# Copying the chunk indicators on GpSimd (POOL) in place of VectorE (DVE), with a new order of every engine's queue

## Chip, cores and metric

One core of one Trainium2 chip. The metric is the device time of one execution in microseconds (us). The core has five engines that run side by side, each through its own list of instructions in order: PE (matrix products and transposes), ACT (activations, copies out of PSUM), DVE (elementwise work, reductions, copies), POOL (GpSimd, here casts, fills and selects) and SP (which issues nearly all DMAs). They wait for one another through semaphores.

## What is computed

Attention over selected chunks of keys, then a gMLP block with a residual. Cut to what matters:

```python
# q, k, v: (4, 8, 768, 64); chunks of 32 keys, nc = 24; top_k = 6
k_min, k_max = k_chunks.min(3), k_chunks.max(3)
ub = sum_d(maximum(q * k_min, q * k_max))         # a bound for each query and chunk
ub = where(chunk is causal, ub, -1e9)
sel = each query's 6 best chunks
scores = where(sel & causal, q @ k.T / 8, -1e9)
x = softmax(scores) @ v                           # heads side by side: (4, 768, 512)

h = gelu(x @ w_in)                                # (4, 768, 1024)
u, v_ = halves of h
v_n = (v_ - mean) / sqrt(var + 1e-6) * g_ln
out = x + (u * (w_sg @ v_n + b_sg)) @ w_out       # w_sg mixes the 768 positions
```

## The kernel before

**Work.** The 32 heads are taken as 16 pairs, p = 0 to 15; four pairs make a batch. The two heads of a pair lie on partitions 0 to 63 and 64 to 127. A pair goes through these steps (the words in brackets are the names that the code gives its operations):

- k and q are loaded, transposed on PE (`ktr`, `qtr`, L550, a half of 384 columns at a time), and copied out of PSUM by ACT or DVE (`kev`, `qev`, L450 on ACT, L453 on DVE). DVE reduces k to its minima and maxima per chunk (`kmm`, L578, four per pair) and subtracts one from the other (`wsub`, L597). The relu of q (`rel`) is done on DVE for pairs 0 to 3 (L619) and on ACT after them (L616); it reads both halves of the pair's qT. POOL casts q to bf16 into QA (`qcast`, L625) and v into vx (`vcast`, L635).
- The bounds are matmuls of q and relu(q) with the minima and differences (`ub`, L660 for pairs 0 to 3 one by one, L707 for later pairs two by two). The first form also reads the small tiles CMw and CMb, which POOL and ACT make at the start. DVE turns the bounds (L670), takes the best eight (L677), marks what lies below the sixth (L683) and turns the marks back into Dt (`dt`, L687).
- Scores are matmuls (`sc`) in pieces of at most 1024 PSUM columns, with two buffers in turn; ACT takes exp of each piece into E (`exp`, L849 for pairs 0 to 3, L801 after). POOL zeroes what lies above the diagonal (`aff`, L858, L806). For pairs 0 to 3 the selection enters the scores as further matmuls of Dt with IND (L840), so nearly every piece of their scores waits for Dt. For later pairs the marks stand in QA and the indicator stands in KA, beside q and k: a DMA (`qd`) brings Dt into QA, a copy of INDF into KA (`mrow`, L749 on DVE) or a DMA does the other.
- PE multiplies E with v (`pv`, L879, then the diagonal blocks `pvd`, L885), and DVE divides by the sums (`rcp`, L895; `xs`, L897) into XS.

After every fourth pair the batch goes through the gMLP: XS is transposed (`xtr`, L919, by DMA for some), x @ w_in (`hv`, L943; `hu`, L962), gelu on ACT, statistics on DVE (L952), a power on POOL (L984), the normalised vhat on DVE (L996), the mixing matmuls (`pt`, L1014), gate and product on DVE (L1031, L1035), the last matmuls (`ou`, L1047), the residual sum on DVE (L1056) and a store. While the first pairs run, w_sg is loaded, cast on POOL (L446), transposed on PE (L496) and copied out by DVE (L453), and w_in and w_out are loaded and cast (L446).

**The indicators.** IND is a bf16 tile of 128 x 2 x 768. On partitions 0 to 31, first plane, its row c is -480 in the 32 columns of chunk c and 0 elsewhere. POOL zeroes the tile (L397), DVE fills 32 rows (L399), POOL cuts them to the chunks with two selects (L401). The same 32 x 768 block is then needed at partitions 32 (plane 1), 64 (plane 0) and 96 (plane 1): three copies, on DVE at L412 when `INDV` is 1. DVE adds the planes to INDF (L417).

**Order.** Every operation gets a number as the program is written down. A table, `TABLE`, lists these numbers for each engine in the order in which the engine runs them, the PSUM buffer of every tile, and how many idle matmuls PE runs ahead of some operations (`filler`: seven ahead of the first transposes of k, four ahead of the first transpose of q, four ahead of the first transpose of pair 1's k). The program works out from the tables which waits are needed. With `shift=True` an operation on POOL also waits for the one ahead of it on POOL, and the one behind waits for it. Buffers that are freed late hold the loads that are to fill them: SP issues in order too.

Some numbers: 13, 14, 15 are the three copies, 16 is INDF; 9, 11, 12 make IND on POOL; 19 is CMw, 20 and 21 are CMb, 8 is identB, 4 to 7 small fills on POOL; 45, 49 are `ktr` and 54, 56 `qtr` of pair 0, 52, 48 its `kev` and 57, 55 its `qev`, 46, 47, 50, 51 its `kmm`, 53 its `wsub`, 58 its `rel`, 59 its `qcast`, 61 its `ub`; 81, 82, 85, 86 are `kmm` of pair 1, 94 its `qcast`. 65, 100, 123, 175 are Dt of pairs 0 to 3.

Of the kernel before, what the change touches and what calls it, by code (L numbers as in the profile page):

```python
# [256 lines left out]
def dmac(issue=530):  # L257
    return issue, issue


def _build(nc, ctx, q, k, v, w_in, g_ln, w_sg, b_sg, w_out, out):
# [4 lines left out]
    NT = S // 128  # L266
# [25 lines left out]
    P = Program()  # L292
# [12 lines left out]
    wsgT = T("wsgT", [128, NT, S], BF16)  # L305
# [17 lines left out]
    WSB = 1  # L323
    WSC = "pool"
# [4 lines left out]
    INDV = 1  # L329
# [51 lines left out]
    def idle(e):  # L381
# [7 lines left out]
         reads=["onesF"], writes=["identF"])  # L389
# [87 lines left out]
    def wsg_load(j):  # L477
# [4 lines left out]
        if WSB:  # L482
            sb = vh0[:, S * (j % 4):S * (j % 4) + S]
            if WSC == "pool":
                cast(sb, dst, S, ("wsc", j), [("stg", j % 4)] + names, [("stb", j % 4)])
            elif WSC == "dve":
                P.op("dve", lambda d: d.tensor_copy(sb, dst), dve(S, rate=2), ("wsc", j), port=True,
                     reads=[("stg", j % 4)] + names, writes=[("stb", j % 4)])
            else:
                P.op("act", lambda d: d.activation(sb, dst, ACTF.Copy), act(S), ("wsc", j),  # L490
                     reads=[("stg", j % 4)] + names, writes=[("stb", j % 4)])
            t = ps_g.tile((0, 1))
# [619 lines left out]
    for p in range(4, NP + 4):  # L1112
# [40 lines left out]
    "act": (  # L1153
# [11 lines left out]
    "dve": (  # L1165
# [99 lines left out]
```

## Time and profile before

| | us |
|---|---|
| median of 3 runs | 213.79 |
| lowest and highest | 213.75, 213.96 |
| the profiled execution | 213.85 |
| its span, first to last instruction | 212.1 |
| ahead of and behind the span | 1.75 |
| granted TensorE clock, share of full speed | 0.999 |

The page gives busy time, share of the span and count of instructions for each engine; its PEld is PE's loading of weights, beside its matmuls. The chain of work that ended last is followed back from the last instruction, at each step to what released it, and gives shares of the span by engine. The table of stretches gives, for each stretch from A to B, its length, the busy us and number of instructions of PE, PEld, DVE, ACT and POOL, PE's clock, the share of the DMA engines and GB/s. A row of the timeline is: start, duration, engine, line of the code, operation, tile written <- tiles read, shape; x3 means three such instructions in a row, and brackets give the engine's idle time ahead of them and what ended it.

### The profile page before, as it was taken

Reading aid. Unit: us, or ns where it says so; the run is one execution under the profiler, and the core shown is the slowest. Engines: PE = TensorE matmul, PEld = TensorE weight load, DVE = VectorE, ACT = ScalarE, POOL = GpSimd, SP = SyncE. Lnnn points to the kernel's source line nnn. Section 1 sums busy time; section 2 is a strip of 40 time slices with the busy share of each in tenths; the row PEclk is TensorE's granted clock in tenths of the full one; section 3 lists DMA queues with packets and bytes.
Section 4 is the critical chain, followed back from the end, with each engine's and each line's share of the span. In section 5 each row is a group of like instructions: output and inputs, shape, how many; then the busy total and the mean of one; then the engine's idle time right before and its main releaser. Section 6 shows DMA issues by size and latency. Waiting matters only on the chain.

```text
span 212.1 us, 5923 instructions
## 1 busy us (share of the span) xinstructions
PE 203.4 (96%) x2326; PEld 134.0 (63%) x2326; DVE 184.1 (87%) x537; ACT 158.5 (75%) x246; POOL 88.8 (42%) x119
## 2 busy tenths in 40 slices
PE   7989999889999999999999999999999999999993
PEld 3646677644767577776456767779646668545552
DVE  2999999879999899898799999899897887788894
ACT  2468999987599779998949989999977868256000
POOL 8424697795262645474121456465502311002000
PEclk9999999999999999999999999999999999999999
DMA  7999999992989998898989988826320007412007
GB/s 152 218 219 254 212 237 336 338 306 68 221 225 231 215 273 205 194 211 189 230 201 220 207 165 220 224 79 149 59 61 3 3 0 97 129 47 105 2 33 264
DMA packets 91339, 36.07 MB, mean 170 GB/s; under 512 B 84144, under 2 KB 86448, under 8 KB 91312
## 3 DMA queue, kind: packets, MB, share of 16 engines
q1 hardware_dynamic: 91024, 35.31, 73.7%
q8 instruction: 18, 0.29, 0.6%
q10 hardware_dynamic: 288, 0.39, 0.5%
q14 instruction: 9, 0.07, 0.1%
HBM read 24.77 MB, written 6.29 MB: 146 GB/s over the span
## 4 chain that ended last, share of the span: by engine, by line
PE 63%; DVE 23%; ACT 9%; issue 2%; POOL 1%; DVEq 0%
PE PSG L1014 15%; PE PSC L795 11%; PE PSG L1047 9%; PE PSG L943 7%; DVE W L578 6%; PE PSG L962 6%; ACT E L801 5%; PE PSG L550 5%; PE PSG L879 4%; DVE vhat L996 3%; DVE XS L897 2%; PE PSG L707 2%; ACT KA L450 2%; PE PSC L382 2%; PE PSG L885 2%
## 5 line engine op out<-in xcount | busy, mean ns | idle before, releaser
L801 ACT ACTIVATE E<-PSC 128x1024 bf16<-128x1024 f32 (+1 forms) x72 | 62.9, 917 | 7.8 <-PE PSC L795 7.6
L795 PE MATMUL PSC<-QA,KA 128*128 128x128 bf16 (+2 forms) x336 | 37.5, 246 | 0.4
L578 DVE TENSOR_REDUCE W<-PSG 128x12 f32<-128x384 f32 x64 | 32.7, 547 | 3.8 <-PE PSG L550 3.6
L1014 PE MATMUL PSG<-wsgT,vhat 128*128 128x384 bf16 x192 | 34.5, 326 | 0.4 <-DVE vhat L996 0.2
L806 POOL TENSOR_SCALAR_AFFINE_SELECT E<-E 128x768 bf16<-128x768 bf16 x24 | 21.1, 878 | 32.3 <-ACT E L801 31.9
L625 POOL CAST QA<-qT 64x768 bf16<-64x768 f32 (+1 forms) x28 | 24.1, 859 | 15.9 <-ACT qT L450 10.0
L795 PEld LDWEIGHTS PSC<-QA,KA 128*128 128x128 bf16 x336 | 24.1, 98 | 8.4 <-ACT E L801 2.4
L1014 PEld LDWEIGHTS PSG<-wsgT,vhat 128*128 128x128 bf16 x192 | 17.9, 98 | 12.5 <-ACT uT L968 1.3
L1047 PE MATMUL PSG<-woutb,uT 128*128 128x512 bf16 (+1 forms) x100 | 23.7, 371 | 0.0
L962 PE MATMUL PSG<-xT,winb 128*128 128x384 bf16 x128 | 23.6, 326 | 0.0
L1031 DVE SCALAR_TENSOR_TENSOR PSG<-PSG,glnT,bsgbc 128x384 f32<-128x384 f32 x32 | 19.7, 619 | 4.1 <-PE PSG L1014 3.9
L849 ACT ACTIVATE E<-PSC 128x1024 bf16<-128x1024 f32 (+3 forms) x26 | 21.2, 866 | 2.4 <-PE PSC L840 2.1
L943 PE MATMUL PSG<-winb,xT 128*128 128x512 bf16 x96 | 22.1, 379 | 0.6 <-issue 0.6
L968 ACT ACTIVATE uT<-PSG 128x384 bf16<-128x384 f32 x32 | 15.1, 490 | 10.0 <-PE PSG L962 9.7
L450 ACT ACTIVATE KA<-PSG 128x384 bf16<-128x384 f32 (+1 forms) x38 | 18.3, 492 | 3.7 <-DVE W L578 3.3
L879 PE MATMUL PSG<-vx,E 128*128 128x65 bf16 x480 | 19.9, 194 | 1.0 <-DVE XS L897 0.6
L635 POOL CAST vx<-vn 128x768 bf16<-128x768 f32 x16 | 13.3, 836 | 17.8 <-DMA vn<-in_v_dram 13.4
L879 PEld LDWEIGHTS PSG<-vx,E 128*128 128x128 bf16 x480 | 17.6, 97 | 3.6 <-DVE XS L897 1.5
L948 ACT ACTIVATE vgb<-PSG 128x512 f32<-128x512 f32 x24 | 13.2, 599 | 7.2 <-PE PSG L943 7.0
L1035 DVE TENSOR_TENSOR uT<-PSG,uT 128x384 bf16<-128x384 f32 x32 | 17.7, 555 | 0.9
L897 DVE TENSOR_TENSOR XS<-PSG,rden 128x384 bf16<-128x384 f32 x32 | 17.7, 554 | 0.9
L952 DVE BATCH_NORM_STATS2 stats<-vgb 128x6 f32<-128x512 f32 x24 | 15.8, 685 | 2.6 <-ACT vgb L948 2.5
(88 smaller groups left out, 328.8 us busy)
## 6 DMA issues: line engine op xcount, KB each, us to landing
kn<-in_k_dram SPq DMA_DIRECT2D x32, 192.0 KB, 4.6
qn<-in_q_dram SPq DMA_DIRECT2D x32, 192.0 KB, 4.5
vn<-in_v_dram SPq DMA_DIRECT2D x12, 384.0 KB, 5.2
out_dram<-osb SPq DMA_DIRECT2D x18, 256.0 KB, 2.4
vn<-in_v_dram SPq DMA_DIRECT2D x8, 192.0 KB, 4.8
uT<-in_moe_w_sg_dram SPq DMA_DIRECT2D x4, 384.0 KB, 6.2
vgb<-in_moe_w_in_dram SPq DMA_DIRECT2D x3, 512.0 KB, 6.1
KA<-INDF SPq DMA_DIRECT2D x12, 96.0 KB, 2.6
```

The source lines that it names most:

```text
L450: P.op("act", lambda e: e.activation(dst(), src(), ACTF.Copy), act(n), tag, reads=reads, writes=writes, ps=ps, shift=shift)
L578: P.op("dve", lambda d, m=m, op=op, src=src, h0=h0, h1=h1: d.tensor_reduce(W[w][:, m, 12 * h0:12 * h1].rearrange("p (h c) -> p h c", h=h1 ...
L625: P.op("pool", lambda g, i=i, r0=r0, r1=r1: g.tensor_copy(QA[w][i or 0][r0:r1, :], qT[r][r0:r1, :]), gps(S, 250 if i == 1 else 150), ("qca ...
L795: r = e.matmul(t.ap()[:, o:o + n], KA[w][i][:, 128 * kb:128 * kb + 128], QA[w][i][:, q0:q0 + n], start=True, stop=True)
L801: P.op("act", lambda e, t=t, c0=c0, c1=c1, i=i: e.activation(E[es][:, i, c0:c1], t.ap()[:, 0:c1 - c0], ACTF.Exp, scale=SCALE), act(c1 - c0 ...
L849: P.op("act", lambda e, t=t, c0=c0, c1=c1, n=n: e.activation(E[es][:, :, c0:c1], t.ap().rearrange("p (i x) -> p i x", i=2)[:, :, 0:n], ACT ...
L879: r = e.matmul(t.ap()[:, 65 * (qb - q0):65 * (qb - q0) + 65], E[es][:, i, at[kb, qb]:at[kb, qb] + 128], vx[w][:, kb, i, :], start=x == 0, ...
L897: P.op("dve", lambda d, pv3=pv3, nq=nq, rs=rs, q0=q0, q1=q1: d.tensor_tensor(XS[:, b % 2, hh // 2, q0:q1, i * DH:(i + 1) * DH], pv3()[:, : ...
L943: r = e.matmul(t.ap()[:, 0:F], xT[s][:, dk, 128 * qt:128 * qt + 128], winb[:, dk, F:DFF], start=(dk == 0), stop=(dk == NDK - 1), skip_grou ...
L962: r = e.matmul(t.ap()[:, 0:TG], winb[:, dk, 128 * fb:128 * fb + 128], xT[s][:, dk, TG * tg:TG * tg + TG], start=(dk == 0), stop=(dk == NDK ...
L1014: r = e.matmul(t.ap()[:, 0:TG], vhat[s][:, sb, 128 * fb:128 * fb + 128], wsgT[:, sb, TG * tg:TG * tg + TG], start=(sb == 0), stop=(sb == N ...
L1047: r = e.matmul(t.ap()[:, 0:n1 - n0], gT[s][:, fb, 128 * qt:128 * qt + 128], woutb[:, fb, n0:n1], start=(fb == 0), stop=(fb == NF - 1))
```

## The change

`INDV` goes from 1 to 2: the three copies of IND become POOL's `tensor_copy` (the branch stands in the code before already), each with `shift=True`. An option `WSD` for transposing w_sg by DMA is added and is off. The tables are new ones for all five engines, with new PSUM buffers, and the fillers stand at the same places in PE's list (two of them now named by the other half of the same transposes). The sets of operations are the same on every engine, but for 13, 14 and 15, which go from DVE's list to POOL's.

```diff
     WSB = 1
+    WSD = 0
     WSC = "pool"
...
-    INDV = 1
+    INDV = 2
...
     "pe": (
-        "1 45 49 54 56 84 80 61 91 188 89 103 107 196 192 96 190 194 166 198 112 114 242 159 200 155 246 250 "
-        "164 119 254 248 244 204 229 227 252 208 209 133 205 309 317 216 221 315 171 319 311 258 259 313 262 "
+        "1 49 45 54 56 80 84 61 91 188 89 103 107 196 192 96 190 194 166 198 112 155 159 242 114 200 164 254 "
+        "250 248 119 244 246 204 205 229 227 252 208 209 133 317 309 221 216 315 171 313 311 137 262 319 263 "
...
     "act": (
-        "22 23 52 55 48 57 83 92 189 90 87 197 193 191 195 199 243 201 247 251 162 255 249 245 158 230 228 "
-        "253 231 310 318 316 224 225 320 219 312 314 220 364 366 370 362 368 284 278 372 273 282 274 279 285 "
+        "23 52 57 55 48 22 83 92 189 90 87 197 193 191 195 199 243 201 255 251 249 158 245 162 247 230 228 "
+        "253 231 318 310 316 225 224 314 219 220 320 312 368 362 273 370 366 364 372 282 278 284 274 279 285 "
...
     "dve": (
-        "0 28 18 10 26 24 17 25 27 47 51 50 14 46 13 15 53 58 85 82 81 86 62 63 88 64 65 110 93 105 106 109 "
-        "16 108 104 97 98 113 99 111 100 167 115 116 160 161 157 165 156 120 121 122 168 163 266 123 210 212 "
-        "134 206 211 207 222 218 223 217 172 173 174 175 138 264 265 260 261 277 276 331 325 326 272 226 271 "
+        "0 25 27 17 18 10 26 28 24 50 51 47 46 53 58 82 85 81 86 62 63 64 88 65 110 93 106 104 105 109 97 16 "
+        "108 98 167 99 113 100 115 111 116 161 157 156 165 160 120 121 163 206 207 122 212 123 266 210 211 "
+        "168 223 218 222 217 134 172 173 138 174 175 264 272 265 260 271 261 276 277 331 325 326 280 226 329 "
...
     "pool": (
-        "9 386 215 334 2 3 269 19 11 4 12 20 21 6 7 5 8 59 94 202 203 213 117 60 169 132 267 233 257 95 256 "
-        "136 232 118 322 321 332 170 79 374 373 73 287 77 71 286 288 384 140 148 152 181 144 457 404 403 353 "
+        "386 9 4 215 2 334 3 20 7 5 11 12 21 13 15 19 8 6 59 14 269 94 202 203 213 117 60 132 169 267 232 257 "
+        "95 136 233 256 332 118 322 321 79 170 374 373 77 73 71 286 152 287 148 384 144 140 288 457 403 183 "
...
     "sp": (
-        "29 30 31 32 34 33 35 36 39 40 69 68 67 42 41 66 37 38 131 128 129 127 43 126 44 135 74 124 75 177 "
+        "29 30 31 32 34 33 35 36 40 39 66 68 42 69 41 67 37 38 131 128 129 126 127 44 43 135 74 75 176 177 "
...
     "filler": (
-        "45:7 54:4 84:4 "),
+        "49:7 54:4 80:4 "),
```

More of the change, by code (lines that the diff above doesn't have):

```diff
@@ L491, in wsg_load @@
                      reads=[("stg", j % 4)] + names, writes=[("stb", j % 4)])
+            if WSD:
+                P.op("sp", lambda e: e.dma_start_transpose(wsgT[:, :, 128 * j:128 * j + 128], sb), dmac(1300), ("wst", j),
+                     reads=[("stb", j % 4)] + [("vhat", 0, x) for x in range(NT)],
+                     writes=[("wsgT", j, hf) for hf in range(2)], dma=f"wt{j}", xfer=900)
+                return
             t = ps_g.tile((0, 1))
@@ L1134 @@
     "pe": (
[18 rows of a table removed]
-    "act": (
[11 rows of a table removed]
-    "dve": (
[18 rows of a table removed]
-    "pool": (
[13 rows of a table removed]
[18 rows of a table added]
+    "act": (
[11 rows of a table added]
+    "dve": (
[18 rows of a table added]
+    "pool": (
[13 rows of a table added]
     "slots": (
-        "0123021232033001111103211301001112301011000111023013323000101132100111010012301010102132032123220323"
-        "3232223333321100112210110011102310011001101032100001100132100101110303223203321332233232232221011013"
-        "2101000001132101010001011330110001110220111010032103310123213323323223233201011032010011320001112311"
-        "010022012320013111020122002331032103"),
+        "1023203010212331111110123201001112230301010011032012323010100123001110101103210010103220122230332323"
+        "2223233323230110013211001011003210000101110132101100100132100001130312022330121223333223322321000102"
+        "2100101111032100110110100321000100101331001101032110201031332332222223333201110022101100320001112311"
+        "000133103120301130012122121333000210"),
     "filler": (
-        "45:7 54:4 84:4 "),
+        "49:7 54:4 80:4 "),
 }
```

98 rows, old and new, of the table TABLE are left out of this document.

## The prediction

> **What bounds the kernel now.** I read the page's busy shares and its chain of work first, then the busy times by stretch, then the timeline of the stretches in which the engines of the chain change.
>
> ```profile
> PE 203.4 (96%) x2326; PEld 134.0 (63%) x2326; DVE 184.1 (87%) x537; ACT 158.5 (75%) x246; POOL 88.8 (42%) x119
> ...
> PE 63%; DVE 23%; ACT 9%; issue 2%; POOL 1%; DVEq 0%
> ```
>
> The shares alone would name PE. The chain says more: 23% of the span, some 49 us, hang on DVE, which is where the change takes work away. The stretches say when; their columns are busy us of PE, PEld, DVE, ACT and POOL.
>
> ```profile
> 5.00:10.00 5.00, 5.00 (x34) 3.40 (x36) 4.23 (x11) 2.19 (x5) 2.44 (x8) 1.00 1.35 218
> ...
> 35.00:40.00 5.00, 4.57 (x92) 3.60 (x92) 4.88 (x10) 5.00 (x7) 3.70 (x6) 1.00 1.08 355
> ...
> 60.00:65.00 5.00, 4.79 (x33) 3.00 (x32) 4.57 (x10) 4.95 (x8) 3.64 (x5) 1.00 0.88 213
> ...
> 200.00:205.00 5.00, 5.00 (x31) 2.84 (x29) 5.00 (x11) 0.00 (x0) 0.00 (x0) 1.00 0.00 2
> ```
>
> From 10 to 40 us DVE is nearly full (4.88 of 5 in the row shown); ACT joins it in the second half (5.00). Late in the kernel PE is full (200 to 205). So there are two kernels in a row: attention of the first pairs, paced by DVE and ACT, up to the first gMLP matmul, then a stage paced by PE. What the first stage saves moves the second one forward whole, as long as PE finds its inputs there; what is saved later off PE is worth nothing. Between 5 and 10 us, where the three copies stand, DVE is not full: 4.23 of 5.
>
> **The three copies.** The timeline of the first 14 us (start, duration, engine, line, operation, tiles):
>
> ```profile
> 4.48 0.82 POOL L401 TENSOR_SCALAR_AFFINE_SELECT IND<-IND 32x768 bf16<-32x768 bf16 x1
> ...
> 5.27 0.91 POOL L426 TENSOR_SCALAR_AFFINE_SELECT CMb<-CMb 64x288 bf16<-64x288 bf16 x2
> 5.66 1.59 DVE L578 TENSOR_REDUCE W<-PSG 128x12 f32<-128x384 f32 x3 [2.97 <-PE PSG L550]
> ...
> 5.98 1.51 PE L382 MATMUL PSC<-warm 128*128 128x512 bf16 x4
> ...
> 7.28 0.35 DVE L412 COPY IND<-IND 32x768 bf16<-32x768 bf16 x1
> ...
> 7.33 0.82 PE L550 MATMUL PSG<-identF,qn 128*128 128x128 f32 x6
> 7.64 0.56 DVE L578 TENSOR_REDUCE W<-PSG 128x12 f32<-128x384 f32 x1
> ...
> 8.23 0.72 DVE L412 COPY IND<-IND 32x768 bf16<-32x768 bf16 x2
> ...
> 8.62 0.49 ACT L450 ACTIVATE qT<-PSG 128x384 f32<-128x384 f32 x1
> ...
> 9.15 0.46 DVE L619 TENSOR_SCALAR rT<-qT 128x576 f32<-128x576 f32 x1
> 9.18 1.11 POOL L625 CAST QA<-qT 128x768 bf16<-128x768 f32 x1 [2.49 <-ACT qT L450]
> 9.52 1.94 DVE L578 TENSOR_REDUCE W<-PSG 128x12 f32<-128x384 f32 x4
> ...
> 10.99 1.73 SPq L528 DMA_DIRECT2D qn<-in_q_dram  x2
> ...
> 12.78 1.11 POOL L625 CAST QA<-qT 128x768 bf16<-128x768 f32 x1 [2.49 <-ACT qT L450]
> ```
>
> *Removed from DVE.* Three copies, 0.35 + 0.72 = 1.07 us. But behind them stands the relu of pair 0 (L619, 9.15), which reads the whole of qT, and ACT writes the second half of that from 8.62 to 9.11. ACT waits there for PE's transposes of q (7.33 to 8.15), and those stand behind four filler matmuls (L382, to 7.49) that the new table keeps in the same place. In the new order ACT takes the halves the other way round and ends at the same 9.11, because the later transpose ends at 8.15 whatever the order. So DVE finishes its four reductions near 7.75 (5.66 and four steps of about 0.52), the 24-column subtraction near 8, and then waits for 9.15: the 1.07 us turn into idle time. The reductions of pair 1 stand behind the relu in both orders and start at 9.52 as before. **I take the copies' removal at nothing.** What is late next there is ACT's qT, and behind it PE's fillers; bounds are 0 and 1.07.
>
> *Added to POOL.* No row shows POOL copying from one group of 32 partitions to another. The nearest row is its select of the same tile (L401, 32x768 bf16 to bf16): 0.82; the dearest 768-element cast is 1.11 (L625). I take 0.82, with 1.11 and, for a form never seen, twice the nearest, 1.64, as the upper end. POOL's rows before them end near 5.8 (the two selects of CMb, L426, end at 6.18 in the old order; the new one has 0.36 less ahead of them: a memset of 0.36 and CMw's select of 0.18 have gone behind, two small memsets of W have come forward), so two copies run from 5.8 to 7.5, then CMw, identB and one small memset until 8.35, then the cast of pair 0 (9.18 as before, since it waits for the same qT). That is 0.83 us of cover, 0.41 for each copy: up to 1.2 us each nothing moves. The third copy stands between that cast and the next one, in an idle 2.49 us less one memset of 0.41. The change makes each copy wait for the POOL instruction before it; that is the order it has anyway. CMw comes later on POOL (7.75 in place of 3.6) and its copy on ACT moves behind four evictions, to about 9.6; the first bound matmul, which reads it, needs the relu, to 9.61. Nothing, then.
>
> [...]
>
> **The new order up to the gMLP.** All engines get another sequence, so I walk it with the durations of the rows.
>
> ```profile
> 18.57 0.56 DVE L453 COPY qT<-PSG 128x384 f32<-128x384 f32 x1
> ...
> 19.53 0.48 DVE L687 STREAM_TRANSPOSE Dt<-Dn 128x288 bf16<-128x288 bf16 x1
> ...
> 26.55 0.48 DVE L687 STREAM_TRANSPOSE Dt<-Dn 128x288 bf16<-128x288 bf16 x1
> ...
> 27.14 0.39 DVE L749 COPY KA<-INDF 64x768 bf16<-64x768 bf16 x1
> ...
> 32.88 0.48 DVE L687 STREAM_TRANSPOSE Dt<-Dn 128x288 bf16<-128x288 bf16 x1
> ...
> 36.55 1.10 DVE L749 COPY KA<-INDF 64x768 bf16<-64x768 bf16 x1
> ...
> 42.85 0.56 DVE L897 TENSOR_TENSOR XS<-PSG,rden 128x384 bf16<-128x384 f32 x1
> ```
>
> ```profile
> 20.79 1.94 ACT L849 ACTIVATE E<-PSC 128x1024 bf16<-128x1024 f32 x2 [0.62 <-PE PSC L840]
> ...
> 27.68 2.90 ACT L849 ACTIVATE E<-PSC 128x1024 bf16<-128x1024 f32 x3
> ...
> 34.77 4.70 ACT L849 ACTIVATE E<-PSC 128x1024 bf16<-128x1024 f32 x5
> ...
> 40.08 0.39 ACT L849 ACTIVATE E<-PSC 128x256 bf16<-128x256 f32 x1
> ```
>
> *Masks.* The masked scores of a pair wait for its Dt (L687: 19.53, 26.55 and 32.88 for pairs 1 to 3). For pair 1 the new order puts one qT eviction ahead of it that stood behind it (0.37 more): Dt at 20.4 in place of 20.0, ACT's next exp at 20.9 in place of 20.79, but a small one comes first, and the half dozen ACT instructions behind it close up again to within 0.1. For pair 2 a reciprocal and a product XS (0.2 + 0.56) come ahead and two small vector instructions and a copy of 0.58 go behind: Dt ends at 27.17 against 27.03; ACT's exps of pair 2 start at 27.93 against 27.68, **0.25 lost**. For pair 3 the eviction of a w_sg block (0.56) comes ahead: Dt ends at 33.9 against 33.4; the exps of pair 3 start at 34.7 against 34.77, since ACT was the later one.
>
> *Gain at the end of the stage.* Before the last exp of pair 3 (40.08) the old order has a q and a k eviction that the new one puts behind it, and the new one has one k eviction instead: about 0.4 less. Five exps at 0.92 and one k eviction after 34.7 bring it to 39.65. POOL's two diagonal selects of pair 3 (0.86 each) now wait for that order's last but one exp, 39.75, and end at 41.5; the last product XS of pair 3 (42.85) ends at 42.75 in place of 43.41. ACT still has five evictions and the relu of pair 5 to do, to 42.85, before the bound matmuls of pairs 4 and 5; transposes, ACT's evictions of them, and the first gMLP matmul follow in the same steps as now.
>
> ```profile
> L446 POOL CAST winb<-vgb 128x1024 bf16<-128x1024 f32 x3 | 3.1, 1039 | 0.1
> ```
>
> ```profile
> 46.06 4.29 PE PSG L943 x19
> ...
> 57.51 2.75 DVE vhat L996 x6
> 60.38 2.11 PE PSG L1014 x12
> ```
>
> PE's first gMLP matmul (46.06) comes at about 45.55: **0.5 gained**. The weight casts it reads (POOL, L446) end at 44.7: after 41.5 three casts of 1.04.
>
> ```profile
> qn<-in_q_dram SPq DMA_DIRECT2D x32, 192.0 KB, 4.5
> ```
>
> ```profile
> 16.97 0.55 PE L550 MATMUL PSG<-identF,qn 128*128 128x128 f32 x3
> ```
>
> *DMA.* Loads are moved too: half of pair 3's q goes from the 11th load to the 14th, an issue in the row of 10.99, so by the 4.5 us of the page it lands at 15.5 to 16.4. PE reads it at 16.97, behind scores that wait for ACT in both orders, so nothing. SP's later loads (w_sg, w_out, q and k of pairs 6 to 8, the mask rows) change places among themselves; those that I followed still land ahead of PE's use.
>
> **The gMLP of batch 0 and after.** DVE's vhat (57.51 to 60.26) holds PE's first mixing matmul until 60.38, and PE is idle for 0.21 of the 5 us from 60 on, which is that wait. In the new order PE has two more small groups ahead of that point and the same work in all, and vhat, behind the last w_sg eviction, the variance and POOL's power, ends within 0.1 us of PE's readiness. So the **0.2** of waiting go. From there PE is full in both; the last 13 us have the same 14 groups and one more that moved in from before them. I take all later moves at zero, which is a choice: I followed them only at the tail and at batch 1's start.
>
> **Sum.** Copies 0, order before the gMLP -0.5, wait before the first mixing matmul -0.2: -0.7 on the profiled execution's 213.85 (span 212.1 and 1.75 around it), 213.15. The median of the runs is 0.06 lower, 213.79: **213.1**.
>
> ```profile
> 23.98 0.63 PE L879 MATMUL PSG<-vx,E 128*128 128x65 bf16 x15
> ...
> 26.76 0.34 PE L885 MATMUL PSG<-vx,E 128*128 128x65 bf16 x6
> ```
>
> ```profile
> 36.40 1.04 POOL L446 CAST winb<-xT 128x1024 bf16<-128x1024 f32 x1
> ```
>
> **Rivals.**
> *The copies count in full* (213.79 - 1.07 = 212.7). For it: DVE is the full engine of the next 30 us. Against: ACT's 9.11 ahead of the relu. 12%.
> *A lock eats the gain* (213.8). DVE's 64-partition copy of the indicator takes 0.39 in one place (27.14) and 1.10 where a POOL cast had just begun (36.55 against 36.40). In the new order one such copy stands directly ahead of pair 2's Dt, at 26.3, and POOL's cast for pair 4 starts at 26.45. If DVE is 0.15 us later than I think, the copy costs 0.7 more, and ACT, which then waits for Dt, passes all of it on: -0.7 + 0.7. 18%. [...]
> *A new wait ahead of a mask* (slower, 214.6). The product XS of head 0 now stands on DVE ahead of pair 2's Dt. It needs head 0's diagonal matmul on PE, at 26.76 to 27.10 in the old order, behind Dt's need. My walk has it done by 24.9, since PE takes it directly after the first part (23.98) and DVE comes by at 25.2. But PE gets there only after a score buffer is freed by ACT. If it ends later than 25.2, DVE, Dt, the scores and ACT wait one for another, us for us; as late as now, 27.1, it costs 1.9: 215.0. From 26.4 on (1.2) it is slower than before by over 0.2%: 214.3 to 215.0, the middle 214.6. 30%. The same form, an order that makes engines wait in a ring, can come anywhere in the 60 to 180 us that I took at zero, so it gets this much.
> *POOL's copies are dear.* Above 1.2 us each, the cast of pair 0 and everything behind it move by twice the excess: 0.9 us at 1.64, 214.0; 9%, half of it within 0.2%, half slower.
>
> **Chances.** My forecast has 31%. Faster by over 0.2% (about what a measurement of this kernel can tell from none, 0.43 us): forecast and first rival, 0.43. Within 0.2%: the lock and half of the dear copies, 0.22. Slower: the rest, 0.35. The forecast's own range is 212.8 to 213.4. The range given reaches from the full copies with a little of the rest, 212.4, to the full price of the new wait, 215.0.
>
> **What would show it.** Three POOL copies of IND, two between 5.8 and 7.5 and one after 10.2, of 0.82 each; DVE idle for about 1.1 us ahead of a relu that still starts near 9.15; the reductions of pair 1 at 9.5. Dt of pairs 1 to 3 ending near 20.4, 27.2 and 33.9. The last XS of pair 3 near 42.75, the first gMLP matmul near 45.5, the first mixing matmul near 59.7 to 60.0. Wrong is: the relu at 8.1 (first rival), an indicator copy of 1.1 us ahead of Dt (second), a gap on DVE ahead of the reciprocal of head 0 (third), POOL copies above 1.2 us (fourth), or PE idle in the later stages by more than now.

## Result and profile after

The changed kernel takes **214.9 us** (median of 11 runs, 214.14 to 216.06) against 213.79 (213.60 to 213.98) before: a ratio of 1.0049, 95% interval 1.0029 to 1.0069. It is slower, where 213.1 was forecast; the range, 212.4 to 215.0, holds the median by 0.1. The profiled execution took 215.11 with a span of 213.1. So 1.0 of its 1.26 us over the old profiled one lies in the span, and the time around the span grew from 1.75 to 2.01.

The page, busy times and chain:

```profile
PE 203.5 (96%) x2326; PEld 134.6 (63%) x2326; DVE 182.9 (86%) x534; ACT 158.6 (74%) x246; POOL 91.8 (43%) x122
...
PE 68%; DVE 16%; ACT 10%; DMA 2%; issue 1%; POOL 1%; SPq 0%; DVEq 0%
```

DVE has 1.2 us less to do than before and POOL 3.0 more; the chain's DVE share fell from 23% to 16%, PE's rose from 63% to 68%. By the chain alone this looks like relief for DVE. The stretches (same columns as before) show where DVE went the other way; the first row is the old kernel's from 30 to 35 us, the others are the changed kernel's:

```profile
30.00:35.00 5.00, 4.91 (x111) 3.48 (x100) 4.56 (x19) 4.85 (x9) 3.76 (x5) 1.00 1.13 288
```

```profile
5.00:10.00 5.00, 4.78 (x26) 3.47 (x26) 2.62 (x7) 2.31 (x6) 3.42 (x8) 1.00 1.15 218
...
25.00:30.00 5.00, 4.94 (x99) 4.03 (x97) 4.83 (x17) 5.00 (x9) 3.03 (x4) 1.00 0.95 229
30.00:35.00 5.00, 4.64 (x93) 3.08 (x88) 4.93 (x19) 4.46 (x8) 3.58 (x6) 1.00 1.15 260
35.00:40.00 5.00, 4.82 (x117) 4.01 (x113) 4.62 (x13) 4.80 (x7) 4.20 (x5) 1.00 0.88 311
...
60.00:65.00 5.00, 4.91 (x43) 3.48 (x42) 4.93 (x11) 4.97 (x8) 3.41 (x5) 1.00 1.10 234
```

Between 5 and 10 us DVE fell from 4.23 to 2.62: the copies, 1.07 of it, left, and the relu and the reductions of pair 1 start 0.36 later in this profile. From 25 to 30 us ACT is full (5.00). From 30 to 35 DVE has 4.93 in place of 4.56, and ACT 4.46 in place of 4.85: ACT waits there. PE has 4.91 in place of 4.79 between 60 and 65. The timeline, first where the copies stood:

```profile
5.84 1.70 POOL L410 COPY IND<-IND 32x768 bf16<-32x768 bf16 x2
...
8.61 0.87 ACT L451 ACTIVATE qT<-PSG 128x384 f32<-128x384 f32 x2 [0.90 <-PE PSG L556]
...
9.51 0.46 DVE L625 TENSOR_SCALAR rT<-qT 128x576 f32<-128x576 f32 x1 [1.18 <-ACT qT L451]
...
10.71 0.82 POOL L410 COPY IND<-IND 32x768 bf16<-32x768 bf16 x1
...
13.36 0.89 POOL L631 CAST QA<-qT 128x768 bf16<-128x768 f32 x1 [1.36 <-ACT qT L451]
13.49 0.80 DVE L603 TENSOR_TENSOR W<-W 128x24 f32<-128x24 f32 x1
...
14.21 0.47 DVE L693 STREAM_TRANSPOSE Dt<-Dn 128x288 bf16<-128x288 bf16 x1
```

POOL's copies are at 5.84 (two, 1.70) and 10.71 (0.82): as forecast. DVE stands idle for 1.18 us ahead of the relu (L625): as forecast too, though the relu itself comes 0.36 later than forecast in this profile, in which the first k landed at 5.18 in place of 4.60. Then something that the prediction never looked at: wsub of pair 1 (L603), 0.17 us long before, takes **0.80**, and stands directly ahead of Dt of pair 0 (L693). It started at 13.49, 0.13 after POOL's cast for pair 1 (L631, 13.36), and ended when that cast had. In the old profile the same two stood like this:

```profile
12.63 0.17 DVE L597 TENSOR_TENSOR W<-W 128x24 f32<-128x24 f32 x1
12.75 0.46 DVE L683 TENSOR_TENSOR Dn<-U,m 128x288 bf16<-128x288 f32 x1
```

wsub came ahead of dn of pair 0 (the marks, L683), and the cast at 12.78, 0.02 before wsub ended. The new order swapped wsub and dn. The same thing comes twice more at the masks of pairs 2 and 3:

```profile
26.83 0.36 DVE L755 COPY KA<-INDF 64x768 bf16<-64x768 bf16 x1
26.91 0.64 POOL L761 MEMSET QA<- 64x384 uint32 x1 [1.93 <-PE PSC L846]
27.20 0.48 DVE L693 STREAM_TRANSPOSE Dt<-Dn 128x288 bf16<-128x288 bf16 x1
...
27.61 0.82 POOL L631 CAST QA<-qT 64x768 bf16<-64x768 f32 x1
27.71 1.02 DVE L755 COPY KA<-INDF 64x768 bf16<-64x768 bf16 x1
...
28.38 1.07 POOL L864 TENSOR_SCALAR_AFFINE_SELECT E<-E 128x768 bf16<-128x768 bf16 x1
...
29.41 0.83 POOL L641 CAST vx<-vn 128x768 bf16<-128x768 f32 x1
29.45 1.10 DVE L625 TENSOR_SCALAR rT<-qT 128x576 f32<-128x576 f32 x1
...
30.47 1.93 DVE L584 TENSOR_REDUCE W<-PSG 128x12 f32<-128x384 f32 x4
```

The indicator copy into KA for pair 5 (L755) starts 0.10 after a cast and takes 1.02; relu of pair 3 (L625) starts 0.04 after the next cast and takes 1.10. In the old order both stood at 25.39 to 26.53, where no POOL cast ran (POOL was idle from 24.93, had a memset of 0.41 at 25.91 and cast again from 26.49):

```profile
25.39 0.45 DVE L619 TENSOR_SCALAR rT<-qT 128x576 f32<-128x576 f32 x1
...
25.95 0.58 DVE L749 COPY KA<-INDF 64x768 bf16<-64x768 bf16 x1
```

The new order also freed two such instructions: the copy that took 1.10 at 36.55 in the old kernel takes 0.42 (38.58), and a wsub that took 0.68 there (38.84) now takes 0.27 together with its neighbour (39.92). But those stand behind the last mask, beside exps of pair 3 that run on without a gap in the old kernel.

Behind the two held ones come the four reductions of pair 4 (30.47), and ACT's evictions behind those:

```profile
31.97 0.98 ACT L451 ACTIVATE KA<-PSG 64x384 bf16<-64x384 f32 x2 [0.49 <-DVE W L584]
...
36.25 1.02 ACT L855 ACTIVATE E<-PSC 128x1024 bf16<-128x1024 f32 x1 [0.20 <-PE PSC L846]
```

```profile
47.09 1.05 PE L949 MATMUL PSG<-winb,xT 128*128 128x512 bf16 x4 [0.61 <-issue]
```

ACT waits 0.49 for DVE's reductions at 31.97, and at 36.25 the exps of pair 3 start, 0.20 later than ACT was free. Dt of pairs 1 to 3 end at 21.04, 27.68 and 35.45 (before: 20.01, 27.03, 33.36). The last product XS of pair 3 ends at 44.44 and the first gMLP matmul comes at 47.09 (before 43.41 and 46.06): 1.0 lost where 0.5 was to be gained. From there the two kernels run nearly alike: PE's last matmul ends at 209.86 against 208.93.

### The profile page after: what moved, and what is told of

The parts are those of the page before. It is cut to its first block, busy times and chain, and to the rows that moved or that the text cites. A ratio compares the mean times of both kernels' runs of the same rounds, so it can differ in the third digit from the quotient of the medians.

```text
span 213.1 us, 5920 instructions
## 1 busy us (share of the span) xinstructions
PE 203.5 (96%) x2326; PEld 134.6 (63%) x2326; DVE 182.9 (86%) x534; ACT 158.6 (74%) x246; POOL 91.8 (43%) x122
## 4 chain that ended last, share of the span: by engine, by line
PE 68%; DVE 16%; ACT 10%; DMA 2%; issue 1%; POOL 1%; SPq 0%; DVEq 0%
PE PSG L1020 14%; PE PSC L801 11%; PE PSG L1053 9%; PE PSG L949 8%; PE PSG L968 7%; PE PSG L556 6%; PE PSG L885 5%; ACT E L807 4%; DVE W L584 3%; PE PSG L713 3%; ACT E L855 2%; DMA kn<-in_k_dram 2%; PE PSG L891 2%; DVE stats L958 2%; DVE m L683 2%; ACT qT L451 1%
## 5 line engine op out<-in xcount | busy, mean ns | idle before, releaser
L801 PE MATMUL PSC<-QA,KA 128*128 128x128 bf16 (+2 forms) x336 | 38.0, 246 | 0.1
L1020 PE MATMUL PSG<-wsgT,vhat 128*128 128x384 bf16 x192 | 34.7, 326 | 0.1
L631 POOL CAST QA<-qT 64x768 bf16<-64x768 f32 (+1 forms) x28 | 23.8, 851 | 14.2 <-ACT qT L451 11.4
L990 POOL TENSOR_TENSOR rstd<-rstd,neghalf 128x6 f32<-128x6 f32 x4 | 5.3, 1329 | 33.1 <-DVE rstd L988 33.1
```

The costliest lines, as they stand in the source:

```text
L631: P.op("pool", lambda g, i=i, r0=r0, r1=r1: g.tensor_copy(QA[w][i or 0][r0:r1, :], qT[r][r0:r1, :]), gps(S, 250 if i == 1 else 150), ("qca ...
L801: r = e.matmul(t.ap()[:, o:o + n], KA[w][i][:, 128 * kb:128 * kb + 128], QA[w][i][:, q0:q0 + n], start=True, stop=True)
L1020: r = e.matmul(t.ap()[:, 0:TG], vhat[s][:, sb, 128 * fb:128 * fb + 128], wsgT[:, sb, TG * tg:TG * tg + TG], start=(sb == 0), stop=(sb == N ...
```

## Experiments

Each time is a median in us, followed by the ratio to the old kernel's runs on the same chip (medians 213.6 to 213.8; three chips in all, so kernels of different groups are compared by these ratios) and its 95% interval. Kernels made from the changed one have its line numbers, the others the old ones. A diff shows the piece of an engine's list that is edited.

### The copies or the order?

b_copies: old order, copies on POOL.

```diff
-    INDV = 1
+    INDV = 2
 dve
-47 51 50 14 46 13 15 53 58
+47 51 50 46 53 58
 pool
-12 20 21 6 7 5 8 59 94
+12 20 21 13 15 6 7 5 8 59 14 94
```

> The old order with the change's named part alone: the three copies of IND on POOL, two behind the selects of CMb and the third behind the first cast, and DVE's list without them. Theory (the copies cost and bring nothing, since DVE waits for ACT's qT at the relu of pair 0 and POOL waits for it too): 213.8, within 0.3 either way; the trace shows about 1.1 us of idle time on DVE ahead of that relu, and the relu near 9.15. Rival 1 (the copies were in the way): 212.7, the relu near 8.1. Rival 2 (the copies on POOL are what made the change slow): 214.9.

213.49; 0.9995 (0.9985 to 1.0005). DVE is idle for 0.93 us ahead of the relu, which starts at 8.90.

a_dve: the changed kernel with DVE's copies.

```diff
-    INDV = 2
+    INDV = 1
 dve
-50 51 47 46 53 58
+50 51 47 14 46 13 15 53 58
 pool
-12 21 13 15 19 8 6 59 14 269
+12 21 19 8 6 59 269
```

> The new order with the copies put back on DVE, at the places among the four reductions where the old order had them. Theory (the order of the other instructions makes the loss): 214.9 as the changed kernel, within 0.5. Rival (the copies on POOL make it): 213.8.

214.75; 1.0050 (1.0032 to 1.0067). With b_copies this settles that the **new order** makes the loss; in both orders the copies, by themselves, move the median by less than their runs spread. a_again, the changed kernel profiled once more:

> The changed kernel once more, unchanged, for a second trace: its times spread over 1.9 us where those of the kernel before spread over 0.4. Theory (instructions of DVE and POOL that exclude each other come in one or the other order, by a few hundredths of a us): the two traces part at an instruction that is long in one and short in the other beside a POOL cast. Rival (the landing of the first loads): they part at the first transposes, and the distance stays as it is there.

214.31, a single run. PE's transposes of the first k start at 4.84 here and at 5.22 in the first profile, relu of pair 0 at 8.71 and 9.51, and all of ACT and DVE behind it runs 0.8 earlier to the exps of pair 3; wsub of pair 1 takes 0.80, the two others 1.02 and 1.10 again. So the theory is wrong: the two traces part at the first transposes, and the same three instructions are long in both. a_base measured it with repeats:

> The changed kernel unchanged, on this chip beside the others. 214.6 to 215.0, spread over more than 1 us; theory: its profile shows wsub of pair 1, the indicator copy for pair 5 and relu of pair 3 at 0.80, 1.0 and 1.1 us, whatever the first load's landing, and its span and the time around it 0.3 more than before's 1.74.

214.52; 1.0043 (1.0026 to 1.0061); the three again 0.80, 1.02, 1.10; time around the span 2.02 to 2.13.

### Ahead of the gMLP or behind?

h_af_br takes the new order up to batch 0's first gMLP matmul (PE 431) and what each engine has begun by then, and the old order for the rest; h_bf_ar the other way round.

```diff
 pe (h_af_br)
 307 359 289 240 424
-431 432 446 426 427 441
+426 427 431 436 432 446
```

> The new order on all five engines up to the first gMLP matmul of batch 0 (with POOL's copies), then the old order to the end. Theory (the loss is made in the front, by DVE instructions that wait for a POOL cast and by what stands behind them): as slow as the changed kernel but for its small gain later, 214.3 to 215.0 against 213.63 before. Rival (the loss is made later, or in the time outside the span, which is 2.0 in the changed kernel and 1.7 in the old one): 213.5 to 213.8.

> The old order (and DVE's copies) up to the first gMLP matmul, then the new order to the end. Theory (front): 213.4 to 213.7, a little under the old kernel, since the new order gains 0.1 to 0.2 between that matmul and PE's last one. Rival (the later stages or the time outside the span): 213.9 to 214.7.

h_af_br 214.14; 1.0029 (1.0016 to 1.0043). h_bf_ar 213.66; 1.0000 (0.9989 to 1.0011). The loss is in the front. What the rest of the new order does is seen at one place: in each trace with the old rest PE waits 0.21 for DVE's vhat ahead of the first mixing matmul, and in none with the new rest. What that is worth is less clear. PE's stretch from the first gMLP matmul to its last matmul (46.02 to 208.64 in h_bf_ar) is 162.62 against 162.87 in the old kernel, but over all traces it is 162.66 to 162.88 with the old rest and 162.39 to 162.92 with the new one. The time around the span is longer in h_bf_ar, 1.76 to 2.02.

### Three DVE instructions beside POOL's casts

a_wsub puts the one back that stands ahead of Dt of pair 0:

```diff
 dve
-86 62 63 64 88 65 110
+86 62 63 88 64 65 110
```

> The changed kernel with one small DVE instruction moved by one place: the subtraction of pair 1 (24 columns, both inputs in SBUF) goes back ahead of the marks of pair 0, where the old order had it. In the changed kernel's trace it took 0.80 us in place of 0.17, beside POOL's cast of pair 1, directly ahead of Dt of pair 0. Theory (DVE was locked out by POOL there, and Dt, the scores and ACT passed the 0.6 on): 214.3, Dt of pair 0 ends 0.6 us earlier, near 14.1. Rival (the first load that landed 0.6 us late makes the loss): 214.9 as before, Dt no earlier for the same landing.

214.33; 1.0030 (1.0020 to 1.0040). Dt of pair 0 ended at 13.19 in place of 13.88 in a_again; 0.3 of that was there at the relu (8.39 and 8.71). From the relu's start to the end of Dt it takes 4.56 to 4.97 us in the traces in which wsub of pair 1 is not held, and 5.17 to 5.31 where it is. But in the trace of a_wsub the 0.7 was gone by 21 us, for another reason:

```profile
18.63 0.85 PE L556 MATMUL PSG<-identF,kn 128*128 128x128 f32 x6 [0.62 <-DVE qT L454]
19.41 0.26 PE L840 MATMUL PSC<-QA,KA 64*128 64x128 bf16 x4
```

```profile
qn<-in_q_dram SPq DMA_DIRECT2D x1, 192.0 KB, 4.4
kn<-in_k_dram SPq DMA_DIRECT2D x1, 192.0 KB, 5.7
```

PE stood 0.62 in front of the transposes of pair 3's k, and the first scores of pair 1 (19.41) behind them. The row names DVE, whose eviction had ended at 18.34; it was the load, which took 5.7 us and landed at 18.54. In the three profiles of the changed kernel it took 4.5 to 4.6 and landed by 17.62; no run shows why. The new order has these transposes ahead of those scores; the old one has them behind.

b_wsub is the reverse: in the old kernel this one instruction goes one place back.

```diff
 dve
-86 62 63 88 64 65 110
+86 62 63 64 88 65 110
```

> The old kernel with a single DVE instruction one place later: wsub of pair 1 behind dn of pair 0, as in the new order. Theory (it then starts while POOL's cast for pair 1 runs and waits for its end): it takes 0.8 to 1.0 us in place of 0.17, Dt of pair 0 ends 0.6 to 0.8 later, ACT's exps of pairs 0 and 1 pass it on, and the time rises by 0.3 to 0.7 over 213.7. Rival (the stage swallows it, as the changed kernel seemed to do from 21 us on): Dt of pair 0 later, first gMLP matmul and time within 0.1 of the old kernel's.

214.48; 1.0034 (1.0022 to 1.0046): 0.7 us more for an instruction of 0.17 that only changed places with its neighbour. Its timeline:

```profile
12.94 0.46 DVE L683 TENSOR_TENSOR Dn<-U,m 128x288 bf16<-128x288 f32 x1
12.97 1.12 POOL L625 CAST QA<-qT 128x768 bf16<-128x768 f32 x1 [2.50 <-ACT qT L450]
13.31 0.80 DVE L597 TENSOR_TENSOR W<-W 128x24 f32<-128x24 f32 x1
...
14.04 0.47 DVE L687 STREAM_TRANSPOSE Dt<-Dn 128x288 bf16<-128x288 bf16 x1
```

The cast runs from 12.97 to 14.09, and wsub, which started 0.34 behind it, ends at 14.11. The first gMLP matmul comes 1.0 later, of which 0.2 were there already at the first load.

a_late adds the two others to a_wsub: the copy for pair 5 behind Dt of pair 3, relu of pair 3 ahead of a reciprocal.

```diff
 dve
-122 212 123 266 210 211 168 223
+122 212 123 168 210 211 223
...
-174 175 264
+174 175 266 264
```

> a_free without its move on PE (the transposes of pair 3's k stay ahead of the first scores of pair 1). Theory (the two DVE instructions beside POOL casts cost most): 213.7 to 213.9 against 214.33 without their move; rival (the move on PE was what mattered): 214.2 to 214.4.

214.00; 1.0012 (1.0003 to 1.0021): 0.33 less than a_wsub, and 0.1 above the expected 213.7 to 213.9.

```profile
26.89 0.42 DVE L625 TENSOR_SCALAR rT<-qT 128x576 f32<-128x576 f32 x1
26.90 1.09 POOL L631 CAST QA<-qT 64x768 bf16<-64x768 f32 x1
...
28.64 1.95 DVE L584 TENSOR_REDUCE W<-PSG 128x12 f32<-128x384 f32 x4 [0.64 <-PE PSG L556]
```

Here the relu starts 0.01 ahead of the cast, takes 0.42, and now POOL's cast takes 1.09 (0.82 above). In these rows the one that starts first is not held. Nor is one that starts at the very end of a cast: copies at 27.14 in the old kernel and 38.58 in the changed one start 0.17 and 0.21 before the recorded end of a cast, and take 0.39 and 0.42. The reductions start 1.8 earlier than in the changed kernel's profile and now wait for PE; Dt of pair 3 ends at 33.71 in place of 34.79 in a_wsub and 34.37 to 35.45 in the changed kernel.

a_ktr is a_wsub with the first score piece of pair 1 (242) back ahead of the transposes of pair 3's k (155, 159); a_free is both, a_late and this move.

```diff
 pe
-112 155 159 242 114
+112 242 155 159 114
```

> Changed kernel with wsub of pair 1 ahead of dn of pair 0 (as in the run that gave 214.33) and, on PE, the first score piece of pair 1 moved back ahead of the transposes of pair 3's k. Theory (those transposes wait for a load that lands at 17.4 to 18.5, and the score piece and ACT's exps wait behind them): the first exp of pair 1 starts at 18.4 to 18.9 in place of 19.7, and the time falls to 213.9 to 214.1. Rival (what is gained there is lost again at the masks of pairs 2 and 3): 214.2 to 214.4.

> As a_ktr, and on DVE the indicator copy into KA for pair 5 moved from behind Dt of pair 2 to behind Dt of pair 3, and relu of pair 3 moved ahead of a reciprocal and a product XS. Theory (these two instructions took 1.02 and 1.10 us beside POOL casts where 0.58 and 0.45 were paid before, which holds up the reductions of pair 4, ACT's eviction behind them and Dt of pair 3): Dt of pair 3 ends at 33.4 to 33.9 in place of 34.7, first gMLP matmul 0.5 to 0.9 earlier, time 213.3 to 213.7. Rival (DVE is the bound there as it is, only the order of its work changes): Dt of pair 3 at 34.3 or later, time within 0.15 of a_ktr.

a_ktr 214.10; 1.0031 (1.0015 to 1.0046): the first exp of pair 1 starts at 18.64 (19.71 in a_wsub), as expected, but in this trace the load had landed at 17.04, so it does not show the move alone. The median gains only 0.2 over a_wsub and the ratio nothing; the two held instructions behind it still take 1.02 and 1.10. a_free **213.71; 1.0001** (0.9992 to 1.0010): there the load landed as late as in a_wsub and a_late (18.60), and the first exp of pair 1 starts at 18.43, so the move does what it should. With the held instructions out of the way it is worth about 0.2 (1.0012 to 1.0001, with intervals that overlap). Dt of pair 3 ends at 33.46. Four moves, of wsub, relu, the indicator copy and one score piece, take back the whole loss.

### What are the copies worth, then?

In the trace of b_copies the relu of pair 0 comes 4.35 us after the first k's landing, in the three with the old front and DVE's copies (the old kernel, h_bf_ar, b_wsub) at 4.54 or 4.55, and in the changed kernel's at 3.75 to 4.33. So the copies were on a path to the relu that the prediction overlooked. DVE's first copy stands ahead of the last reduction of pair 0, ACT's eviction of that k waits for the reduction, and ACT's eviction of q stands behind that one. In h_bf_ar the reduction ends at 8.16, the evictions start at 8.19 and 8.58, and ACT has waited 0.08 for the reduction. In the old kernel's own profile this path and PE's transposes of q tie: the reduction ends at 8.20, and the eviction of k (8.25) follows one of q (7.86), for which ACT had waited 0.09 for PE. Two kernels with the old order, and only ACT's list changed:

```diff
 act
-52 55 48 57 83
+52 55 57 48 83
```

b_relu_dve keeps the copies on DVE, b_relu has them on POOL as b_copies.

> The old kernel (copies on DVE) with one ACT instruction moved: the first eviction of pair 0's k behind both evictions of its q, as in the new order. Theory (with DVE's copies the last two of them end near 8.95 and wsub of pair 0 at 9.15, whatever ACT does): relu of pair 0 stays at 4.5 after the landing of the first k, time 213.6 to 213.8. Rival (only ACT's order held the relu): relu 0.3 to 0.8 earlier and the time below 213.4.

> The same move on ACT with the three copies on POOL (as in b_copies, which gave 213.49). Theory (now neither DVE nor ACT's order holds the relu, only PE's transposes of q, which come early or late with PE's slow first matmuls): relu 3.7 to 4.35 after the landing of the first k, Dt of pair 0 earlier by 0.2 to 0.8 and all behind it too, time 213.0 to 213.4, and a wider spread than the old kernel's. Rival (a load or ACT is the next bound, as in the changed kernel): 213.4 to 213.6, as b_copies.

b_relu 213.39; **0.9989** (0.9980 to 0.9998): relu at 8.24, Dt of pair 0 at 13.21, 0.3 to 0.9 earlier than in b_copies and the old kernel, and PE's last matmul ends at 208.44 (208.93). A part of that is PE's first matmuls, which were faster in this profile (0.88 for the six transposes of the first k, against 1.50 in b_copies and 1.54 in the old kernel; see the last section): h_best, below, with the same front and first transposes as slow as the old kernel's (1.54), has the relu at 8.59. The runs spread no wider than the old kernel's, which the theory had wrong. b_relu_dve 214.20; 1.0026 (1.0013 to 1.0038): 0.5 slower than expected. The relu didn't stay at 4.5 after the landing, it came at 4.83, since ACT's earlier q releases POOL's cast earlier:

```profile
7.94 0.72 DVE L412 COPY IND<-IND 32x768 bf16<-32x768 bf16 x2
...
8.31 1.03 POOL L625 CAST QA<-qT 128x768 bf16<-128x768 f32 x1 [1.64 <-ACT qT L450]
8.67 0.71 DVE L597 TENSOR_TENSOR W<-W 128x24 f32<-128x24 f32 x1
9.30 0.45 DVE L619 TENSOR_SCALAR rT<-qT 128x576 f32<-128x576 f32 x1
```

The two DVE copies (7.94 to 8.66) hold wsub of pair 0 until the cast runs (8.31), and then the cast holds wsub, 0.71 for 0.18. With this order of ACT's, taking the copies off DVE is worth 0.8 us (214.20 to 213.39); with the old one nothing that could be measured.

free_dve asks the same in a_free:

```diff
-    INDV = 2
+    INDV = 1
```

(with the copies at the places that they have in a_dve)

> a_free with the three copies back on DVE. Theory (the copies are free on either engine): dt of pair 0 within 0.15 of a_free's 13.13; the time around the span falls from 2.05 to 1.83, as it did when the changed kernel got DVE's copies, so 213.45 to 213.6. Rival (POOL's copies help once the relu isn't late): 0.2 to 0.5 slower than a_free, 213.9 to 214.2.

214.08; 1.0014 (1.0001 to 1.0028). The time around the span did fall to 1.77 to 1.85, but the ratio rose from a_free's 1.0001, by 0.3 us. That speaks for the rival; the intervals still overlap a little. The traces do not show where the 0.3 comes from: Dt of pair 0 ended 0.4 later than in a_free, but PE's first transposes took 1.54 us there and 0.88 in a_free, and by Dt of pair 2 free_dve's trace is ahead (26.55 and 26.73).

### A version that beats both

h_best is b_relu up to the first gMLP matmul and the new order from there.

> b_relu up to the first gMLP matmul, then the new order (h_bf_ar gave 213.66 and PE's last matmul 0.25 earlier behind the first gMLP matmul). Theory: b_relu less 0.25, plus 0.1 to 0.3 of time around the span, 212.9 to 213.4. Rival (the later stage finds its inputs no earlier): 213.5 to 213.8.

**213.31; 0.9984** (0.9975 to 0.9993), 0.3 to 0.5 us under the old kernel on the same chip, by the ratio and by the medians. Against b_relu the 0.08 is too little to tell. PE's last matmul ends at 208.26 (before 208.93), and the time around the span is 1.70 to 1.77.

## Why the prediction was wrong

**Order up to the gMLP: -0.5 forecast, +0.2 to +1.0 seen.** This is the step that failed: the walk with "the durations of the rows", and what it left out.

*Walked with durations from another place.* "For pair 3 ... the exps of pair 3 start at 34.7, since ACT was the later one": they started at 35.17 (a_base), 35.45 (a_again) and 36.25 (first profile). The walk gave each moved instruction the duration that it had in its old place. wsub of pair 1, the copy for pair 5 and relu of pair 3 took 0.80, 1.02 and 1.10 in place of 0.17, 0.58 and 0.45 in their new places: 1.7 us of DVE time, in each of three profiles. It is shown by undoing and by doing: the ratio falls from 1.0043 (a_base) to 1.0030 (a_wsub) and 1.0012 (a_late), and b_wsub alone raises it to 1.0034. wsub of pair 1 wasn't in the walk at all, nor the transposes of pair 3's k ahead of pair 1's scores (a_late to a_free, about 0.2). With all four undone the first gMLP matmul comes at 45.87, 0.2 ahead of the old kernel's and not 0.5; what took the rest is not shown.

*The gain at the end of the stage* was there: from the start of pair 3's exps to the end of the last one the old kernel took 5.70 (34.77 to 40.47), the changed one 5.37 (36.25 to 41.62). That is 0.33 of the 0.4 that the walk had. It was lost ahead of that.

**The second rival was the right mechanism at the wrong place.** It had a copy held by a POOL cast ahead of Dt of pair 2; that copy came at 26.83 with 0.36, ahead of POOL's memset (26.91) and of the cast (27.61). The hold was looked for at one instruction instead of at every DVE instruction that had changed places with a POOL cast. Not only copies are held: wsub, which subtracts one part of W from another, took 0.80 beside the cast in b_wsub and 0.17 without it in the old kernel, and relu of pair 3 took 1.10 beside a cast and 0.45 without. Which other instructions hold one another is not shown.

**Copies removed: 0 forecast.** In the old order that holds in size (b_copies, 0.9995), but the reason given was only half of it. ACT's evictions hung not on PE's transposes alone but also on the reduction behind the first copy (ACT waited 0.08 for it in h_bf_ar). In the new order the relu came earlier than 9.15 in two of three profiles (8.28, 8.71; 9.51 in the first profile), and wsub's 0.63 took that back; a_late and a_free, without the hold, kept it until Dt of pair 0 (13.07 and 13.13 against 13.72). It is not shown that the copies' removal did this: with the copies on DVE the new order has the relu at 8.80 and 8.97 (a_dve, free_dve).

**Copies added: as forecast**, 0.82 each, 1.70 for two.

**Wait before the first mixing matmul: -0.2 forecast.** The wait went, as forecast: the first mixing matmul starts at 61.53 with no wait ahead of it. What PE gained by it is not resolved: from the first gMLP matmul to the last matmul h_bf_ar took 0.25 less than the old kernel, and the changed kernel's three profiles 0.0 to 0.3 less (47.09 to 209.86, the first, is 162.77), while traces with the old rest differ by 0.2 among themselves.

**The new wait (third rival, 30%) did not come**: the reciprocal of head 0 started at 25.64, 0.02 after DVE was free.

**Not in the sum at all:** the time around the span, which the sum took over at 1.75 and which is 2.0 to 2.1 in all runs of the changed kernel against 1.7 to 1.8. It is as short as in the old kernel in b_copies, b_relu and h_best, 1.8 to 1.9 in the new order with DVE's copies (a_dve, free_dve), and between 1.76 and 2.02 in h_af_br and h_bf_ar. Neither the copies nor one half of the order makes it alone; the page shows nothing of it, and its cause stays open. It is 0.3 of the loss, and a_free still pays it (2.01 to 2.09). Open too is why the changed kernel's runs lie 1.9 us apart. A part comes with the first load and PE's first matmuls: in its three profiles the relu comes at 9.51, 8.71 and 8.28 and the first gMLP matmul at 47.09, 46.50 and 46.23. The runs of a_late, a_free and h_best lie 0.5 to 0.6 apart, which speaks for the held instructions, but free_dve's lie 1.5 apart without them, which speaks against.

## What to carry to other kernels

When an order changes, look up for each DVE instruction that moved which POOL instruction runs beside it in its new place, above all ahead of a result that others wait for; a duration from the old place holds only with what ran beside it there (one copy went from 0.58 us to 1.02, another from 1.10 to 0.42). An instruction that is longer than its like and ends with the end of another engine's, in a profile that names no wait, may be such a hold: exchange it with its neighbour and see. And follow a "free" removal through every engine in between: here DVE's copy held DVE's own relu by way of ACT.

## What the runs showed of the hardware

In these traces PE's first matmuls run at two speeds, and the moment of the change differs between profiles of one and the same kernel. The same six f32 transposes of the first k and the idle matmuls behind them, in three kernels (the changed one's first profile, a_late, a_free):

```profile
5.22 1.54 PE L556 MATMUL PSG<-identF,kn 128*128 128x128 f32 x6 [0.38 <-DMA kn<-in_k_dram]
6.56 1.36 PE L383 MATMUL PSC<-warm 128*128 128x512 bf16 x4
```

```profile
4.65 1.01 PE L556 MATMUL PSG<-identF,kn 128*128 128x128 f32 x6
5.50 1.03 PE L383 MATMUL PSC<-warm 128*128 128x512 bf16 x4
```

```profile
4.71 0.88 PE L556 MATMUL PSG<-identF,kn 128*128 128x128 f32 x6
5.42 1.03 PE L383 MATMUL PSC<-warm 128*128 128x512 bf16 x4
```

They take 0.88 to 1.54, the four idle matmuls behind them 1.03 to 1.36 (1.51 in the old profile), while the clock column of the old kernel's profile and of the changed one's first shows 1.00 for the whole first 10 us. a_late and a_free differ in nothing that runs before 15 us, and the three profiles of the changed kernel itself have 1.54, 1.42 and 1.18 for the six transposes. In these three the idle matmuls start 0.43 us apart at first and 0.22 later, the transposes 0.21 and 0.11; the change comes at about 7.2, 5.9 and 5.3 us. What sets that moment is not shown. With the copies on POOL the relu came at 3.5 to 4.35 after k's landing, in the changed kernel's three profiles at 4.33, 3.92 and 3.75. In the three profiles with the old front it came at 4.54 or 4.55, but there the transposes took 1.51 to 1.54 each time, so no profile shows what a fast start would have brought the old kernel.
